# Eight weight pieces summed ahead for the half unit, all by VectorE, and one set of token parts from unit 2 on

## The chip, the cores and the metric

The kernel runs on one core of a Trainium2 chip. The metric is the device time of one execution, in microseconds (us). In the profile PE is TensorE (PEld its weight loads), DVE is VectorE, ACT is ScalarE, POOL is GpSimd and SP is SyncE. All times in the text without a unit are us, and times such as 598.83 count from the start of the span of the profiled execution.

## What is computed

Three stages follow each other: an attention with pooled keys, a mixture of experts with a capacity, and two plain layers over all 2304 tokens. The change is in the last stage, which uses 512 features and 2048 hidden units:

```python
h = x @ w_in            # 512 -> 2048
r = np.maximum(h, 0.0)
g = s * (r * r) + b
out = g @ w_out         # 2048 -> 512
```

A token that its expert had no room for enters the last stage as zeros, so its output row is known without a matmul. Only the kept tokens go through the two layers; the kernel learns their number on the chip.

## The kernel before

**Units.** `last_layers` takes the kept tokens in units of 256 (`CU`). Units 0 and 1 are interleaved in `pair`. Unit 2 is always run. Each later unit stands in a branch: `rest` asks whether more than `u * 256 + 128` tokens are kept and runs `unit(u)` if so; otherwise, if more than `u * 256` are kept, it runs `half(u)` for the last 128 or fewer. With these inputs units 0 to 4 run whole and a half unit ends the program.

**Precision.** A float32 operand is split into a high part `h` that TensorE takes at its fast rate and a low part `l`, and three products (hh, hl, lh) replace one. `w_in` lies in SBUF as 16 pieces `win[f]`, each a pair of high and low parts (in `w1h`/`w1l` for f below 8, in `w2h`/`w2l` above). The tokens of a unit come in as `yr`; `split_y` makes their parts, the high one on ACT (L1032), the low one by `eng` (L1033, POOL when `tokens(u + 1)` calls it). There are two sets of token parts in `x.yp`: set 0 in the tile `yhl`, set 1 in the tiles `y1h` and `y1l`.

**A whole unit.** The first layer makes 16 blocks of 128 hidden units, one for each piece: 12 matmuls into one of four PSUM banks (`ph`: tq, misc, bank2, bank3; L1040). `square` takes a bank by ACT (relu, L1424) and DVE (times itself, L1425) into one of four buffers `rt`; `parts` splits that, with the high part `gh` by ACT (L1439) and the low part `gl` by POOL (L1442, two instructions). Then the second layer runs over two blocks of 128 tokens (L1449), and `store` adds the bias on DVE (L1456) and scatters the rows with an indirect DMA from POOL (L1457).

**The half unit.** For 128 tokens the kernel doesn't use split operands in the first layer: it multiplies plain float32, four matmuls for each of the 16 pieces (L1568), which needs each piece of `w_in` whole. `whole(f)` sums its two parts into a slot (L1560, 128x512 elements). There are three slots, `raw2`, `raw3` and `c_f1`. Unit 2 fills them with pieces 0 to 2 ahead of its second layer, and `half` sums piece f + 3 into the slot of piece f as soon as the matmuls of f have read it. Of these sums the even ones go to DVE and the odd ones to POOL, where they stand between the low parts of `parts`. Each engine does its instructions in the order in which the code issues them.

**What orders the work.** The order is written out by hand (`manual_schedule`); the framework only adds the semaphores. `x.yr`, the four banks and the four `rt` are reused in rotation.

Of the kernel before, what the change touches and what calls it, by code (L numbers as in the profile page):

```python
# [7 lines left out]
F32 = mybir.dt.float32  # L8
# [12 lines left out]
DM = H * D  # L21
# [3 lines left out]
P = 128  # L25
# [864 lines left out]
class Experts:  # L890
# [137 lines left out]
        nc.sync.dma_start(out=self.it[u % 4], in_=self.idc[u * CU:u * CU + CU].rearrange("(j p) o -> p (j o)", p=P))  # L1028

    def split_y(self, u, k, eng):  # L1030
        h, l = self.yp[u % 2]
        self.nc.scalar.copy(h[:, k], self.yr[:, k])  # L1032
        eng.tensor_sub(l[:, k], self.yr[:, k], h[:, k])  # L1033

    def layer1_y(self, u, p, wh, wl):
        n = 0
        yh, yl = self.yp[u % 2]
        for k in range(KD):
            for l, r in ((wh, yh), (wh, yl), (wl, yh)):
                self.nc.tensor.matmul(p[:, :CU], lhsT=l[:, k], rhs=r[:, k], start=n == 0, stop=n == 3 * KD - 1)  # L1040
                n += 1
# [328 lines left out]
def last_layers(nc, tc, c, a, pool, side, x, ps, out):  # L1370
# [4 lines left out]
    w2h, w2l, it, kept, raw, rt = x.w2h, x.w2l, x.it, x.kept, x.raw, x.rt  # L1375
# [12 lines left out]
    sums, more, spare, slots = {}, [], [], []  # L1388

    v8 = lambda z: z.rearrange("p (k c) -> p k c", k=KD)  # L1390
    win = [(x.w1h[:, f], x.w1l[:, f]) for f in range(KF)] + [(v8(w2h[f]), v8(w2l[f])) for f in range(KF)]
# [22 lines left out]
    def conv(n, end=len(steps)):  # L1414
        for _ in range(n):
            if done[0] < end:
                z, i = steps[done[0]]
                z.step(i)
                done[0] += 1

    def square(f, p, n, inside=False):

        r = rt[f % 4][:, :n]
        nc.scalar.activation(r, p, AF.Relu)  # L1424
        nc.vector.scalar_tensor_tensor(out=p if inside else r, in0=p, scalar=0.0, in1=r, op0=ALU.max, op1=ALU.mult)  # L1425

    def place(f, u=0):

        if u != 1 or HEAD <= f < KF2 - 2:
            f -= HEAD if u == 1 else 0  # L1430
            return gh[:, f], gl[:, f]
        t = spare[f % (KF2 - 2)] if f < 3 or f > HEAD else more[(f - 3) // 2][:, (f - 3) % 2]
        return t[:, 0], t[:, 1]

    def parts(f, n=CU, u=0, p=None):

        h, l = place(f, u)
        r = rt[f % 4][:, :n] if p is None else p
        nc.scalar.copy(h[:, :n], r)  # L1439
        if p is None:  # L1440
            for z in (slice(0, n // 2), slice(n // 2, n)):
                nc.gpsimd.tensor_sub(l[:, z], r[:, z], h[:, z])  # L1442
        else:
            nc.vector.tensor_sub(l[:, :n], r, h[:, :n])

    def layer2(p, j, f, c=slice(0, DM), u=0):
        h, l = place(f, u)
        for i, (g, z) in enumerate(((h, 0), (h, 1), (l, 0))):
            nc.tensor.matmul(p[:, c], lhsT=g[:, j * P:j * P + P], rhs=wo[f][:, z, c], start=f == 0 and i == 0, stop=f == KF2 - 1 and i == 2)  # L1449
# [12 lines left out]
    def tokens(u):  # L1462
        if u < NV:
            for k in range(KD):
                x.split_y(u, k, nc.gpsimd)
# [8 lines left out]
    def load_out(i):  # L1474
        nc.sync.dma_start(out=wo[i].rearrange("p c two -> p (c two)"), in_=wout[:, i])

    def pair():

        for i in range(KF2 - 2):
            load_out(i)  # L1480
            if i == 5:
                x.load_y(1)
                for j, n in enumerate(("moe2_s", "moe2_b")):
                    nc.sync.dma_start(out=sb[:, j:j + 1], in_=a[n].unsqueeze(0).to_broadcast([P, 1]))
        more.extend(side.tile([P, 2, 2, CU], F32R, name=f"wo{i}") for i in range(KF2 - 2, KF2))
        spare.extend(x.w.tile([P, 2, CU], F32R, name=f"raw{i}") for i in range(3))
        held = []

        def first(u, f0, f1, banks):
            for n, f in enumerate(range(f0, f1)):  # L1490
                p = banks[f % len(banks)][:, :CU]
                if u or f >= EARLY:
                    x.layer1_y(u, p, *win[f])
                inside = f % 3 == 2
                square(f, p, CU, inside)
                conv(f < 6 or f % 2 if u == 0 else 1 if f < HEAD else 1 + f % 2, steps_of_first)
                if u == 0 and 7 <= f < 7 + KD:
                    x.split_y(1, f - 7, nc.vector)
                if held:
                    parts(*held.pop())  # L1500
                held.append((f, CU, u, p if inside else None))
            parts(*held.pop())

        def second(u, f0, f1, end):
            for f in range(f0, f1):
                for j in range(2):
                    layer2(po[2 * u + j], j, f, u=u)
                conv(1 if u and f < HEAD else 2, end)

        steps_of_first, all_steps = cvs[0].total, len(steps)  # L1510
        conv(2 * FIRST)
        nc.gpsimd.memset(onesf, 1.0)
        first(0, 0, KF2, ps)
        first(1, 0, HEAD, ph)
        x.load_y(2)
        second(0, 0, HEAD, steps_of_first)
        second(1, 0, HEAD, steps_of_first)
        for i in range(KF2 - 2, KF2):
            wo[i] = place_out(i, [P, DM, 2], I32)
            load_out(i)  # L1520
        first(1, HEAD, KF2, ph)
        second(0, HEAD, KF2, all_steps)
        tokens(2)
        second(1, HEAD, KF2, all_steps)
        conv(all_steps)
        raw[0:3] = [x.w.tile([P, DM], F32, name=f"raw{i}") for i in range(3)]
        slots.extend(raw[2:4] + [x.w.tile([P, DM], F32, name="c_f1")])
        sums["drop"] = x.w.tile([P, DM], F32, name="c_u0")

    def unit(u):  # L1530
        if u == 2:
            pair()
        if u + 1 < NV:
            x.load_y(u + 1)
        for f in range(KF2):
            p = ph[f % 4][:, :CU]
            x.layer1_y(u, p, *win[f])
            square(f, p, CU)
            if f:
                parts(f - 1)  # L1540
            if u == 2:
                if f == 1:
                    rows(ph[(f + 3) % 4])
                elif f > 11:
                    store((f - 12) // 2, f % 2, po[f - 12])
        parts(KF2 - 1)
        tokens(u + 1)
        if u == 2:
            for f in range(len(slots)):
                whole(f)  # L1550
        for j in range(2):
            p = po[2 * (u % 2) + j]
            for f in range(KF2):
                layer2(p, j, f)
            store(u, j, p)

    def whole(f):

        if f < KF2:
            (nc.gpsimd if f % 2 else nc.vector).tensor_add(v8(slots[f % len(slots)]), win[f][0], win[f][1])  # L1560

    def half(u):

        for f in range(KF2):
            p = ph[f % 4][:, :P]
            w = slots[f % len(slots)].rearrange("p (k c) -> p k c", k=KD)
            for k in range(KD):
                nc.tensor.matmul(p, lhsT=w[:, k], rhs=x.yr[:, k, 0:P], start=k == 0, stop=k == KD - 1)  # L1568
            square(f, p, P)
            whole(f + len(slots))  # L1570
            if f:
                parts(f - 1, P)
        parts(KF2 - 1, P)

        ids = x.ids_half
        for i in range(2):
            nc.vector.tensor_scalar(out=ids[:, i:i + 1], in0=it[u % 4][:, 0:1], scalar1=2, scalar2=i, op0=ALU.mult, op1=ALU.add)
        for i in range(2):
            c = slice(i * DM // 2, (i + 1) * DM // 2)
            p = po[2 * (u % 2) + i]  # L1580
            for f in range(KF2):
                layer2(p, 0, f, c)
            rows_out(raw[0], p, c, out.rearrange("t (i c) -> (t i) c", i=2), ids[:, i:i + 1])
# [67 lines left out]
```

## Time and profile before

| what | us |
|---|---|
| median of 3 runs | 645.44 |
| lowest and highest run | 642.06 and 647.37 |
| the profiled execution | 640.99 |
| its span, first to last instruction | 639.2 |
| the half unit, first matmul to the end of the span | 598.83 to 639.2 |

The mean granted TensorE clock of the profiled execution is 0.968 of full speed (2.4 GHz). A page gives averages over three different stages; what counts for the change is the last 40 us and the stretch from 443 to 466 in unit 2, so these are read from the timelines of each engine, where a number in brackets is idle time ahead of an instruction and the name behind it is what ended that.

### The profile page before, as it was taken

To read this page: it belongs to the slowest core of one execution; us is meant where nothing else is said; L and a number is where in the kernel's file an instruction comes from. 1 tells how busy PE (TensorE), PEld (TensorE's weight loads), DVE (VectorE), ACT (ScalarE), POOL (GpSimd) and SP (SyncE) were. 2 spreads that over 40 slices of the span, in tenths; PEclk is the share of its full clock that TensorE was granted. 3 is DMA by queue.
4 is the path that set the end of the run, shared out by engine and by line. 5 is a ranking of instruction groups with operands and counts; after the bars stand their busy time and mean duration, and the time that the engine had idled before them with its cause. 6 is when DMAs were issued, how large, how long until landed. Compare 5 with 4: busy or idle time off the path is not lost. (4 is left out here: it accounts for less than half of the span.)

```text
span 639.2 us, 11276 instructions
## 1 busy us (share of the span) xinstructions
PE 582.6 (91%) x4005; PEld 539.6 (84%) x4005; DVE 367.0 (57%) x893; ACT 250.0 (39%) x614; POOL 289.3 (45%) x486
## 2 busy tenths in 40 slices
PE   5788989699899979998899898999999999999885
PEld 5777878589899969997899787799899898898775
DVE  4687898887978966672669999324221031131140
ACT  1445655536456635525336534124033042041130
POOL 6557634716253806113237505227446055164391
PEclk8799999799899979999999999999999999999998
DMA  8999786636749893856587020145200101000000
GB/s 167 181 190 186 156 219 210 214 104 236 236 139 302 276 336 121 258 174 217 168 271 297 1 67 2 33 156 191 67 17 16 36 17 34 33 2 18 21 2 20
DMA packets 67951, 86.12 MB, mean 135 GB/s; under 512 B 24713, under 2 KB 40073, under 8 KB 67856
## 3 DMA queue, kind: packets, MB, share of 16 engines
q1 hardware_dynamic: 57168, 71.04, 37.7%
q10 hardware_dynamic: 8240, 7.14, 3.7%
q0 software_dynamic: 2448, 6.82, 3.4%
q8 instruction: 42, 0.69, 0.4%
q14 instruction: 53, 0.43, 0.2%
HBM read 68.09 MB, written 17.58 MB: 134 GB/s over the span
## 5 line engine op out<-in xcount | busy, mean ns | idle before, releaser
L1442 POOL TENSOR_TENSOR gl<-rt,gh 128x128 fp32r<-128x128 f32 (+1 forms) x192 | 89.3, 488 | 77.6 <-ACT gh L1439 77.4
L1449 PE MATMUL bank<-wo,gh 128*128 128x512 f32 (+1 forms) x340 | 99.8, 377 | 0.4 <-DVE wo L1400 0.4
L936 POOL TENSOR_TENSOR w1l<-kraw,w1h 128x128 fp32r<-128x128 f32 x96 | 51.6, 570 | 50.1 <-ACT w1h L929 50.1
L1113 PE MATMUL bank<-hs,w2h 128*128 128x288 f32 (+1 forms) x308 | 68.6, 311 | 5.1 <-issue 4.7
L1449 PEld LDWEIGHTS bank<-wo,gh 128*128 128x128 f32 x340 | 62.0, 188 | 13.4 <-DVE wo L1400 1.1
L1449 PE MATMUL bank<-wo,gl 128*128 128x512 f32 (+1 forms) x170 | 63.8, 375 | 0.0
L1456 DVE SCALAR_TENSOR_TENSOR raw<-bank,sb,c_u 128x512 f32<-128x512 f32 (+1 forms) x14 | 9.9, 711 | 85.6 <-PE bank L1449 85.6
L1113 PEld LDWEIGHTS bank<-hs,w2h 128*128 128x128 f32 x308 | 50.8, 192 | 6.1 <-issue 5.5
L1424 ACT ACTIVATE rt<-tq 128x256 f32<-128x256 f32 (+1 forms) x26 | 9.5, 367 | 111.7 <-PE tq L1040 89.0
L1113 PE MATMUL bank<-hs,w2l 128*128 128x288 f32 (+1 forms) x148 | 44.9, 303 | 0.0
L944 POOL DMA_INDIRECT xg<-xd,u_idx x23 | 26.1, 1135 | 35.8 <-DVE lt L294 16.4
L1425 DVE SCALAR_TENSOR_TENSOR rt<-bank,rt 128x256 f32<-128x256 f32 (+1 forms) x53 | 21.2, 400 | 36.5 <-ACT rt L1424 36.2
L1439 ACT CAST gh<-rt 128x256 fp32r<-128x256 f32 (+1 forms) x96 | 36.7, 382 | 11.3 <-DVE rt L1425 7.5
L1457 POOL DMA_INDIRECT out_dram<-raw,it x12 | 11.9, 994 | 62.8 <-DVE raw L1456 62.4
L1449 PEld LDWEIGHTS bank<-wo,gl 128*128 128x128 f32 x170 | 31.9, 188 | 6.4
L1424 ACT ACTIVATE rt<-bank 128x256 f32<-128x256 f32 (+1 forms) x60 | 22.3, 371 | 36.7 <-PE bank L1040 27.7
L230 PE MATMUL sc<-kbd,qT 128*128 128x144 f32 (+1 forms) x152 | 25.4, 316 | 6.4 <-DVE rmine L380 3.1
L967 PE MATMUL bank<-xs,w1h 128*128 128x288 f32 (+1 forms) x120 | 27.3, 313 | 2.1 <-DVE hs L970 2.1
L230 PEld LDWEIGHTS sc<-kbd,qT 128*128 128x128 f32 (+1 forms) x152 | 21.8, 200 | 8.5 <-issue 5.9
L1113 PEld LDWEIGHTS bank<-hs,w2l 128*128 128x128 f32 x148 | 28.4, 192 | 0.0
L1425 DVE SCALAR_TENSOR_TENSOR rt<-tq,rt 128x256 f32<-128x256 f32 (+1 forms) x24 | 9.6, 399 | 31.4 <-ACT rt L1424 31.4
L940 DVE TENSOR_TENSOR w2l<-vraw,w2h 128x512 fp32r<-128x512 f32 x39 | 26.8, 686 | 0.9 <-ACT w2h L939 0.5
(496 smaller groups left out, 1729.3 us busy)
## 6 DMA issues: line engine op xcount, KB each, us to landing
kraw<-in_moe_w_dram SPq DMA_DIRECT2D x14, 1024.0 KB
vraw<-in_moe_w_dram SPq DMA_DIRECT2D x14, 1024.0 KB
c_raw<-in_moe_w_in_dram ACTq DMA_DIRECT2D x13, 512.0 KB
wo<-in_moe_w_out_dram SPq DMA_DIRECT2D x13, 512.0 KB
kraw<-in_k_dram SPq DMA_DIRECT2D x8, 576.0 KB
out_dram<-c_u SPq DMA_DIRECT2D x1, 4608.0 KB
q<-in_q_dram SPq DMA_DIRECT2D x16, 256.0 KB
xd<-xr SPq DMA_DIRECT2D x16, 256.0 KB
```

The lines of the kernel that those rows point to most:

```text
L230: nc.tensor.matmul(sc[:n, p // 2, p % 2 * 144:p % 2 * 144 + 144], lhsT=q[:, p, :n], rhs=kbd[b % 2][:, p], start=True, stop=True)
L936: eng.tensor_sub(self.w1l[:, i, z], self.w1(i)[:, z], self.w1h[:, i, z])
L940: eng.tensor_sub(self.w2l[i], self.w2r[:, i], self.w2h[i])
L944: self.nc.gpsimd.indirect_dma_start(out=dst, out_offset=None, in_=self.xd[:have], in_offset=bass.IndirectOffsetOnAxis(ap=idx[:n], axis=0), ...
L967: self.nc.tensor.matmul(p, lhsT=l[:, f, k], rhs=r[k], start=n == 0, stop=n == 3 * KD - 1)
L1113: nc.tensor.matmul(py[d][:, :v.n], lhsT=l[f][:, d * P:d * P + P], rhs=r[f], start=f == 0 and i == 0, stop=f == KF - 1 and i == 2)
L1424: nc.scalar.activation(r, p, AF.Relu)
L1425: nc.vector.scalar_tensor_tensor(out=p if inside else r, in0=p, scalar=0.0, in1=r, op0=ALU.max, op1=ALU.mult)
L1439: nc.scalar.copy(h[:, :n], r)
L1442: nc.gpsimd.tensor_sub(l[:, z], r[:, z], h[:, z])
L1449: nc.tensor.matmul(p[:, c], lhsT=g[:, j * P:j * P + P], rhs=wo[f][:, z, c], start=f == 0 and i == 0, stop=f == KF2 - 1 and i == 2)
L1457: i = nc.gpsimd.indirect_dma_start(out=dst, out_offset=bass.IndirectOffsetOnAxis(ap=ids, axis=0), in_=o[:, c], in_offset=None, bounds_chec ...
```

## The change

Eight slots replace three: `c_f0`, `c_f1`, the storage of `y1h` and `y1l` cut into two slots each, and `raw2`, `raw3`. Unit 2 sums pieces 0 to 7 ahead, and the half unit sums pieces 8 to 15, all on DVE. To free the storage of `y1h` and `y1l`, set 1 of the token parts serves unit 1 alone; units 2 and later all use set 0. The low part in `parts` is cut in pieces of 128 columns, which is as before for 256 tokens and is one instruction rather than two for the 128 of the half unit.

```diff
--- before.py
+++ after.py
@@ -1028,13 +1028,13 @@
         nc.sync.dma_start(out=self.it[u % 4], in_=self.idc[u * CU:u * CU + CU].rearrange("(j p) o -> p (j o)", p=P))
 
     def split_y(self, u, k, eng):
-        h, l = self.yp[u % 2]
+        h, l = self.yp[u == 1]
         self.nc.scalar.copy(h[:, k], self.yr[:, k])
         eng.tensor_sub(l[:, k], self.yr[:, k], h[:, k])
 
     def layer1_y(self, u, p, wh, wl):
         n = 0
-        yh, yl = self.yp[u % 2]
+        yh, yl = self.yp[u == 1]
         for k in range(KD):
             for l, r in ((wh, yh), (wh, yl), (wl, yh)):
                 self.nc.tensor.matmul(p[:, :CU], lhsT=l[:, k], rhs=r[:, k], start=n == 0, stop=n == 3 * KD - 1)
@@ -1438,8 +1438,8 @@
         r = rt[f % 4][:, :n] if p is None else p
         nc.scalar.copy(h[:, :n], r)
         if p is None:
-            for z in (slice(0, n // 2), slice(n // 2, n)):
-                nc.gpsimd.tensor_sub(l[:, z], r[:, z], h[:, z])
+            for z in range(0, n, P):
+                nc.gpsimd.tensor_sub(l[:, z:z + P], r[:, z:z + P], h[:, z:z + P])
         else:
             nc.vector.tensor_sub(l[:, :n], r, h[:, :n])
 
@@ -1524,7 +1524,11 @@
         second(1, HEAD, KF2, all_steps)
         conv(all_steps)
         raw[0:3] = [x.w.tile([P, DM], F32, name=f"raw{i}") for i in range(3)]
-        slots.extend(raw[2:4] + [x.w.tile([P, DM], F32, name="c_f1")])
+        slots.extend(x.w.tile([P, DM], F32, name=f"c_f{i}") for i in range(2))
+        for n in "hl":
+            z = pool.tile([P, 2, DM], F32, name=f"y1{n}")
+            slots.extend(z[:, i] for i in range(2))
+        slots.extend(raw[2:4])
         sums["drop"] = x.w.tile([P, DM], F32, name="c_u0")
 
     def unit(u):
@@ -1557,7 +1561,7 @@
     def whole(f):
 
         if f < KF2:
-            (nc.gpsimd if f % 2 else nc.vector).tensor_add(v8(slots[f % len(slots)]), win[f][0], win[f][1])
+            nc.vector.tensor_add(v8(slots[f % len(slots)]), win[f][0], win[f][1])
 
     def half(u):
```

The first place is DVE in unit 2, from the last two stores of unit 1 to the branch behind the unit (`raw` and `c_f` are slots here, L1560 of before is L1564 of the changed kernel). Before:

```order
L1456 SCALAR_TENSOR_TENSOR raw2_17954<-bank6_1946,sb_17059,c_u0_17956 128x512
L1425 SCALAR_TENSOR_TENSOR rt3_1971<-bank3_1943,rt3_1971 128x256
L1456 SCALAR_TENSOR_TENSOR raw3_1963<-bank7_1947,sb_17059,c_u0_17956 128x512
L1560 TENSOR_TENSOR raw2_17954<-w1h_144,w1l_145 128x512
L1560 TENSOR_TENSOR c_f1_17955<-w1h_144,w1l_145 128x512
L1456 SCALAR_TENSOR_TENSOR raw0_17952<-bank4_1944,sb_17059,c_u0_17956 128x512
L1456 SCALAR_TENSOR_TENSOR raw1_17953<-bank5_1945,sb_17059,c_u0_17956 128x512
```

And now:

```order
L1456 SCALAR_TENSOR_TENSOR raw2_17954<-bank6_1946,sb_17059,c_u0_17959 128x512
L1425 SCALAR_TENSOR_TENSOR rt3_1971<-bank3_1943,rt3_1971 128x256
L1456 SCALAR_TENSOR_TENSOR raw3_1963<-bank7_1947,sb_17059,c_u0_17959 128x512
L1564 TENSOR_TENSOR c_f0_17955<-w1h_144,w1l_145 128x512
L1564 TENSOR_TENSOR c_f1_17956<-w1h_144,w1l_145 128x512
L1564 TENSOR_TENSOR y1h_17957<-w1h_144,w1l_145 128x512 x2
L1564 TENSOR_TENSOR y1l_17958<-w1h_144,w1l_145 128x512 x2
L1564 TENSOR_TENSOR raw2_17954<-w1h_144,w1l_145 128x512
L1564 TENSOR_TENSOR raw3_1963<-w1h_144,w1l_145 128x512
L1456 SCALAR_TENSOR_TENSOR raw0_17952<-bank4_1944,sb_17059,c_u0_17959 128x512
L1456 SCALAR_TENSOR_TENSOR raw1_17953<-bank5_1945,sb_17059,c_u0_17959 128x512
```

Six more sums stand between the stores of unit 1 and those of unit 2, and the sum that wrote `raw2` first now stands last but one.

The second place is DVE in the half unit that runs, from its branch on (`rt` are the squares, L1425). Before:

```order
L1599 COMPARE_AND_BRANCH
L1425 SCALAR_TENSOR_TENSOR rt0_1968<-tq_1607,rt0_1968 128x128
L1425 SCALAR_TENSOR_TENSOR rt1_1969<-misc_1608,rt1_1969 128x128
L1560 TENSOR_TENSOR raw3_1963<-w1h_144,w1l_145 128x512
L1425 SCALAR_TENSOR_TENSOR rt2_1970<-bank2_1942,rt2_1970 128x128
L1425 SCALAR_TENSOR_TENSOR rt3_1971<-bank3_1943,rt3_1971 128x128
L1560 TENSOR_TENSOR raw2_17954<-w1h_144,w1l_145 128x512
L1425 SCALAR_TENSOR_TENSOR rt0_1968<-tq_1607,rt0_1968 128x128
L1425 SCALAR_TENSOR_TENSOR rt1_1969<-misc_1608,rt1_1969 128x128
```

And now:

```order
L1603 COMPARE_AND_BRANCH
L1425 SCALAR_TENSOR_TENSOR rt0_1968<-tq_1607,rt0_1968 128x128
L1564 TENSOR_TENSOR c_f0_17955<-w2h0_146,w2l0_147 128x512
L1425 SCALAR_TENSOR_TENSOR rt1_1969<-misc_1608,rt1_1969 128x128
L1564 TENSOR_TENSOR c_f1_17956<-w2h0_146,w2l0_147 128x512
L1425 SCALAR_TENSOR_TENSOR rt2_1970<-bank2_1942,rt2_1970 128x128
L1564 TENSOR_TENSOR y1h_17957<-w2h_1951,w2l_1952 128x512
L1425 SCALAR_TENSOR_TENSOR rt3_1971<-bank3_1943,rt3_1971 128x128
L1564 TENSOR_TENSOR y1h_17957<-w2h_1951,w2l_1952 128x512
L1425 SCALAR_TENSOR_TENSOR rt0_1968<-tq_1607,rt0_1968 128x128
```

Before, a sum stood behind every second square, and the slot that it wrote was read three pieces later; now one stands behind each of the first eight squares, and the slot that it writes is read eight pieces later.

The third place is POOL in the half unit (`gl` are the low parts). Before:

```order
L1599 COMPARE_AND_BRANCH
L1560 TENSOR_TENSOR raw2_17954<-w1h_144,w1l_145 128x512
L1442 TENSOR_TENSOR gl_17067<-rt0_1968,gh_17066 128x64 x2
L1560 TENSOR_TENSOR c_f1_17955<-w1h_144,w1l_145 128x512
L1442 TENSOR_TENSOR gl_17067<-rt1_1969,gh_17066 128x64 x2
L1442 TENSOR_TENSOR gl_17067<-rt2_1970,gh_17066 128x64 x2
L1560 TENSOR_TENSOR raw3_1963<-w1h_144,w1l_145 128x512
L1442 TENSOR_TENSOR gl_17067<-rt3_1971,gh_17066 128x64 x2
L1442 TENSOR_TENSOR gl_17067<-rt0_1968,gh_17066 128x64 x2
```

And now:

```order
L1603 COMPARE_AND_BRANCH
L1442 TENSOR_TENSOR gl_17067<-rt0_1968,gh_17066 128x128
L1442 TENSOR_TENSOR gl_17067<-rt1_1969,gh_17066 128x128
L1442 TENSOR_TENSOR gl_17067<-rt2_1970,gh_17066 128x128
L1442 TENSOR_TENSOR gl_17067<-rt3_1971,gh_17066 128x128
L1442 TENSOR_TENSOR gl_17067<-rt0_1968,gh_17066 128x128
L1442 TENSOR_TENSOR gl_17067<-rt1_1969,gh_17066 128x128
```

Seven sums have left POOL's row, and the low part of each block is one instruction.

## Rows read from the trace of the kernel before

**Rows 1.** The chain that ended last, from 601 to 605: start, us, what.

```profile
601.03 1.64 issue
...
602.88 1.42 POOL raw L1560
...
604.34 1.30 PE bank L1568 x8
```

**Rows 2.** Timeline of PE, half unit: start, us, instruction, [idle before <-releaser].

```profile
598.83 1.05 PE L1568 MATMUL tq<-yr,raw 128*128 128x128 f32 x8
...
604.34 1.30 PE L1568 MATMUL bank<-yr,raw 128*128 128x128 f32 x8 [2.67 <-POOL raw L1560]
...
608.75 1.95 PE L1568 MATMUL bank<-yr,raw 128*128 128x128 f32 x16
610.53 1.06 PE L1568 MATMUL tq<-yr,c_f 128*128 128x128 f32 x8
...
620.31 1.16 PE L1568 MATMUL bank<-yr,raw 128*128 128x128 f32 x8 [0.73 <-POOL raw L1560]
621.22 0.48 PE L1449 MATMUL bank<-c_raw,gh 128*128 128x256 f32 x2
```

**Rows 3.** Windows: length, busy us of PE, PEld, DVE, ACT, POOL, PEclk, DMA share, GB/s.

```profile
606.00:609.00 3.00, 3.00 (x18) 3.00 (x17) 1.18 (x3) 0.68 (x4) 3.00 (x7) 0.56 0.00 0
...
615.00:618.00 3.00, 2.27 (x20) 2.08 (x20) 2.11 (x5) 0.93 (x4) 3.00 (x6) 1.00 0.00 0
```

**Rows 4.** Timeline of POOL, half unit.

```profile
602.88 1.41 POOL L1560 TENSOR_TENSOR raw<-w1h,w1l 128x512 f32<-128x512 f32 x1 [1.84 <-ACT rt L1424]
...
608.88 1.80 POOL L1442 TENSOR_TENSOR gl<-rt,gh 128x64 fp32r<-128x64 f32 x4
...
613.43 1.26 POOL L1560 TENSOR_TENSOR c_f<-w2h,w2l 128x512 f32<-128x512 f32 x1
...
622.12 1.16 POOL L1442 TENSOR_TENSOR gl<-rt,gh 128x64 fp32r<-128x64 f32 x4 [0.20 <-ACT gh L1439]
```

**Rows 5.** Timeline of DVE, half unit.

```profile
602.28 0.29 DVE L1425 SCALAR_TENSOR_TENSOR rt<-misc,rt 128x128 f32<-128x128 f32 x1 [1.61 <-ACT rt L1424]
602.48 0.68 DVE L1560 TENSOR_TENSOR raw<-w1h,w1l 128x512 f32<-128x512 f32 x1
603.08 0.28 DVE L1425 SCALAR_TENSOR_TENSOR rt<-bank,rt 128x128 f32<-128x128 f32 x1
...
609.55 0.68 DVE L1560 TENSOR_TENSOR c_f<-w2h,w2l 128x512 f32<-128x512 f32 x1
...
613.76 1.48 DVE L1560 TENSOR_TENSOR raw<-w2h,w2l 128x512 f32<-128x512 f32 x1
```

**Rows 6.** Timeline of ACT, half unit.

```profile
600.90 0.28 ACT L1424 ACTIVATE rt<-misc 128x128 f32<-128x128 f32 x1 [0.62 <-PE misc L1568]
```

**Rows 7.** Timeline of POOL, end of unit 2 and start of unit 3.

```profile
448.04 0.90 POOL L1442 TENSOR_TENSOR gl<-rt,gh 128x128 fp32r<-128x128 f32 x2
448.88 3.77 POOL L1033 TENSOR_TENSOR y1l<-yr,y1h 128x256 fp32r<-128x256 f32 x4
...
469.06 0.87 POOL L1442 TENSOR_TENSOR gl<-rt,gh 128x128 fp32r<-128x128 f32 x2 [1.69 <-ACT gh L1439]
```

**Rows 8.** Timeline of POOL, end of the first layer of unit 4.

```profile
579.35 2.81 POOL L1033 TENSOR_TENSOR yhl<-yr,yhl 128x256 fp32r<-128x256 f32 x4
```

**Rows 9.** Timeline of DVE, second layer of unit 2.

```profile
447.79 1.71 DVE L1560 TENSOR_TENSOR raw<-w1h,w1l 128x512 f32<-128x512 f32 x1 [3.02 <-DMA out_dram<-raw,it]
...
454.28 0.75 DVE L1456 SCALAR_TENSOR_TENSOR raw<-bank,sb,c_u 128x512 f32<-128x512 f32 x1 [3.64 <-PE bank L1449]
465.38 0.75 DVE L1456 SCALAR_TENSOR_TENSOR raw<-bank,sb,c_u 128x512 f32<-128x512 f32 x1 [10.34 <-PE bank L1449]
```

**Rows 10.** Timeline of PE, second layer of unit 2 and the start of unit 3.

```profile
453.85 0.39 PE L1449 MATMUL bank<-wo,gl 128*128 128x512 f32 x1
...
465.18 0.28 PE L1040 MATMUL tq<-y1h,w1h 128*128 128x256 f32 x1
```

## The prediction

> **What bounds the kernel now.** I read the chain that ended last first, backwards from the end. Where the half unit begins it runs over POOL: 1.64 in which POOL waited for nothing shown, a sum of two weight parts (L1560) of 1.42, and only then TensorE [rows 1]. So the place is the half unit's first layer. Its 16 pieces run from 598.83 to 621.22, 22.39 us [rows 2]. A piece that waits for nothing takes 0.89 (two from 608.75 to 610.53), so 16 of them need 14.24. **8.1 us are lost**, and TensorE's rows say to what: 2.67 idle before the fourth piece until POOL's sum had ended, later 0.73 before every second piece for the same reason [rows 2], and slow pieces in between, as the granted clock fell to 0.56 (near the 1.2 GHz level) in 606 to 609 after the long wait and was back at 1.00 later [rows 3].
>
> Why POOL is late: its timeline is without a gap from 602.88 to 623.28 [rows 4]. Of the 13 sums that the half unit makes, the seven odd ones are POOL's, about 1.26 each, with the low parts of two blocks between them. That is a period of about 2.8 for two pieces where TensorE needs 1.78. DVE takes 0.68 for the same sum when nothing blocks it [rows 5] and has gaps.
>
> **The change, part by part.**
>
> *Sums leave POOL in the half unit.* Seven sums go, 7 × 1.26 = 8.8 of POOL's time. The low part of a block becomes one instruction of 128 columns, which costs 0.44 (0.87 for two in unit 3 [rows 7]) in place of 2 × 0.29 (1.16 for four at the very end [rows 4]). POOL's load per piece falls to 0.44 against TensorE's 0.89, so POOL stops being the bound.
>
> *Eight slots instead of three.* Pieces 0 to 7 are ready before the half unit starts, so no TensorE wait for a sum is left there. Piece 8 + k is summed right behind square k. On DVE a square costs 0.20 to the next issue (602.28 to 602.48) and a sum 0.60 (602.48 to 603.08) [rows 5]: 0.80 per piece, below 0.89. A sum has eight pieces, 7.1 us, of lead over its reader; all eight take 6.4. What is late next is not the sum but the *square behind it*: it frees the PSUM bank for the piece four later. If DVE starts no earlier than in this trace (602.28), square k ends at about 602.4 + 0.8k, and piece k + 4 can start on time at 598.83 + 0.89 × (k + 4) = 602.4 + 0.89k: just ahead for k = 1 and further ahead after. The first layer then ends at 598.83 + 14.24 = 613.1, 8.1 earlier, and the clock has no long wait to fall after.
>
> *Who follows.* The second layer reads the low parts. In this trace the last of them was ready at 623.28, 2.06 after that layer had begun [rows 2, 4], and TensorE didn't wait; POOL, less loaded, will not be later. Second layer, last store and drain (621.22 to 639.2) only move forward.
>
> *Unit 2 makes eight sums on DVE, not two, and POOL one less.* DVE waited 3.02 for a scatter to land before it could write raw2, and idled 3.64 and 10.34 before the unit's two stores [rows 9]. Now the first six slots wait for nothing, so the sums start at 444.8 and need 8 × 0.68 = 5.4 free, or 8 × 1.71 = 13.7 if all are blocked like the first in this trace. They end between 450.2 and 458.5. The store behind them, at 454.28, may slip by 4.2; its bank is next wanted two units later, and DVE's next task is at 465.38. Cost 0. For POOL: beside two DVE sums its four token parts took 3.77, without them 2.81 [rows 7, 8], so 0.48 lost per sum, 8 × 0.48 = 3.9. POOL's last low part of the unit ends at 448.94 and TensorE wants it at 453.85, 4.9 later [rows 7, 10]; the token parts, 452.65 + 3.9 = 456.5, are wanted at 465.18. Cost 0, with 1.0 to spare in the worse place.
>
> *One set of token parts.* The parts of unit u + 1 are now written over those of unit u. They are made behind the last square of unit u, which itself waited for the last matmul that reads them. The wait that this adds is already over: 0. The 128-column cut leaves 256-token units as they are.
>
> *Sum.* At most 8.1. TensorE's wait at 601.5 to 604.34 also hid whatever its own code might have come late by; DVE, behind the same branch, got going again only at 602.28, so 0 to 0.8 may show up there. I take the middle, 0.4. **Gain 7.7**: the profiled execution would be 640.99 − 7.7 = 633.3 and the median 645.44 − 7.7 = **637.7**. (The profiled execution lies 4.45 under the median of the runs; I carry the gain over to the median, as the half unit is the same work in each run.)
>
> **The port.** DVE's sum at 613.76 took 1.48, not 0.68: POOL's sum ran from 613.43 to 614.69, and DVE's ended 0.55 after that. But the sum at 609.55, amid four low parts, took 0.68, and those four took 1.80 rather than 1.16 [rows 4, 5]. So either may hold the other up. The Trainium skill ("SBUF — State Buffer", Who interferes with whom) says just this: a VectorE instruction with two SBUF inputs and a GpSimd instruction that reads SBUF exclude each other for a whole instruction, whoever comes first. It speaks against giving every sum to DVE while POOL keeps its low parts: were POOL always first, the gain would be the first rival's 5.3; were DVE always first, the forecast's 7.7. The trace bears out both orders.
>
> **Rivals.**
>
> *DVE becomes the bound.* If each sum finds a low part in flight it costs 0.60 + 0.44, and with the square 1.24 per piece, over TensorE's 0.89. Then square 8, behind eight sums, ends at 602.28 + 8 × 1.24 + 0.1 = 612.3, pieces 12 to 15 follow it, and the layer ends at 612.3 + 4 × 0.89 = 615.9: gain 5.3. POOL also starts with up to two low parts of backlog, 0.9: gain 4.4. If DVE isn't late at the start (from 600.67), 6.9. Time 638.5 to 641.0, say 639.3. For it: the row at 613.76. Against it: a low part can start only after ACT has read the square, when DVE's sum is already running, as at 609.55.
>
> *The code behind the branch comes late.* DVE had its relu at 601.18 [rows 6] and was free, yet squared at 602.28; POOL stood 1.64 with nothing to wait for [rows 1]. If TensorE or DVE loses another such 1.6 where no wait covers it: gain 6.1, time 639.3. The Trainium skill ("Runtime: NRT & Kernel Launch", Instruction fetch mechanics) says that a taken branch out of the loaded window forces a fetch; this trace has the delay but doesn't prove the cause. Code sizes shift by a few instructions, so it may fall elsewhere.
>
> *Slower: unit 2's sums starve POOL.* If each of the eight kept POOL out for the 1.71 that the longest lasted, the last low part would come at 448.94 + 13.7 = 462.6, 8.8 after TensorE wants it; with the slow clock after such a wait (1.7 in the half unit: three pieces from 604.34 in 4.41, not 2.68) 10.5 are lost and 7.7 gained: 648.2. It decides from 4.9 lost by POOL on, and turns the sign from about 11. Against it: the measured 0.48 per sum.
>
> *It doesn't do what it says:* the slots are there but a reader still waits, as for a slot's old content. Unit 2's sums have 140 us of lead, so only the second eight could; no time gained, 645.
>
> **How the numbers follow.** About 1% (6.45 us) is what a measurement can tell from no change here, and 7.7 is 1.2%. Chances: forecast (gain 7.3 to 8.1) 0.62; DVE bound 0.18; late code 0.12; nothing gained 0.05; slower 0.03. The forecast lands over 1% in some 85 of 100 cases, given runs that spread by 5.3; the next two in about 40. Faster 0.62 × 0.85 + 0.30 × 0.4 = 0.65, slower 0.03, same 0.32. Range: from 637.3 less the 3.4 by which the lowest run before lay under the median, 633.9, to DVE's worst, 641.0. All of it is one sign.
>
> **What would show it.** Right: no L1560 (now L1564) row on POOL; 16 pieces in 14.2 to 15 us with granted clock 1.00; POOL with gaps in the half unit; sums of 0.6 to 1.2. Wrong: TensorE waiting on a square (DVE) between pieces 5 and 12; a gap before the fourth piece with no engine to wait for; a TensorE wait on POOL's low parts near 453 in unit 2. It would also be wrong if the stages ahead of unit 2, which the change leaves alone, moved.

## The result and the profile after

| | median, us | runs | ratio to before (95% interval) |
|---|---|---|---|
| before | 643.91 | 642.06 to 647.37 | |
| changed | 634.71 | 633.17 to 636.45 | 0.9862 (0.9827 to 0.9897) |

The kernel is 8.9 us faster (643.91 × 0.0138), with an interval of 6.6 to 11.1. Two later sets of runs of the same kernel gave 0.9836 (0.9787 to 0.9886) and 0.9916 (0.9885 to 0.9948); the three, weighted by the inverse square of their interval's width, make 0.9882, a gain of 7.6. The forecast was 7.7.

One count ahead of the prediction is off by one: units 0 to 5 run whole, the half unit is number 6, and [rows 8] are of unit 5. No term depends on it.

The profiled execution of the changed kernel took 635.53 us (span 633.8). The chain that ended last no longer passes through POOL in the half unit's first layer (start, us, what); compare [rows 1].

```profile
600.82 0.92 PE tq L1572 x8
...
602.63 1.79 PE bank L1572 x16
...
613.45 1.80 PE bank L1572 x16
```

The timeline of TensorE in the half unit, as [rows 2], shows why: the 16 pieces run from 600.65 to 614.99, 14.34 us instead of 22.39. No row has idle time in front; at 604.25, the fifth piece, the wait for the first square's bank costs some 0.1.

```profile
600.65 1.08 PE L1572 MATMUL tq<-yr,c_f 128*128 128x128 f32 x8
...
604.25 1.16 PE L1572 MATMUL tq<-yr,y1l 128*128 128x128 f32 x8
...
613.29 1.95 PE L1572 MATMUL bank<-yr,raw 128*128 128x128 f32 x16
614.99 0.48 PE L1449 MATMUL bank<-c_raw,gh 128*128 128x256 f32 x2
```

The windows of that stretch (length, busy us of PE, PEld, DVE, ACT, POOL, granted clock, DMA share, GB/s) answer to [rows 3]: TensorE is busy throughout, the granted clock stays at 1.00 (the 2.4 GHz level), and of the other engines DVE is now the fullest.

```profile
604.20:608.00 3.80, 3.80 (x35) 3.77 (x35) 3.80 (x9) 2.17 (x10) 2.11 (x4) 1.00 0.01 4
608.00:612.00 4.00, 4.00 (x38) 4.00 (x38) 3.64 (x10) 2.44 (x12) 2.45 (x5) 1.00 0.00 0
```

POOL in the half unit, as [rows 4]: low parts of 0.45 to 0.62, with gaps, the last one done at 617.17, 2.18 after the second layer began.

```profile
604.77 0.45 POOL L1442 TENSOR_TENSOR gl<-rt,gh 128x128 fp32r<-128x128 f32 x1 [1.91 <-ACT rt L1424]
605.46 0.62 POOL L1442 TENSOR_TENSOR gl<-rt,gh 128x128 fp32r<-128x128 f32 x1 [0.24 <-PE tq L1572]
...
607.29 0.52 POOL L1442 TENSOR_TENSOR gl<-rt,gh 128x128 fp32r<-128x128 f32 x1 [0.35 <-PE bank L1572]
...
616.71 0.46 POOL L1442 TENSOR_TENSOR gl<-rt,gh 128x128 fp32r<-128x128 f32 x1 [0.32 <-POOL gl L1442]
```

DVE in the half unit, as [rows 5]: its first square stands 2.30 idle, though the relu that it needs ended at 602.14; from there it runs through its eight sums without a gap, 0.80 to 0.98 per piece and mostly 0.86. A sum starts shortly before POOL's low part ends (607.62, the low part at 607.29 + 0.52 = 607.81).

```profile
603.91 0.29 DVE L1425 SCALAR_TENSOR_TENSOR rt<-tq,rt 128x128 f32<-128x128 f32 x1 [2.30 <-ACT rt L1424]
604.11 0.68 DVE L1564 TENSOR_TENSOR c_f<-w2h,w2l 128x512 f32<-128x512 f32 x1
604.71 0.28 DVE L1425 SCALAR_TENSOR_TENSOR rt<-misc,rt 128x128 f32<-128x128 f32 x1
...
607.62 0.74 DVE L1564 TENSOR_TENSOR y1l<-w2h,w2l 128x512 f32<-128x512 f32 x1
```

Unit 2, as [rows 9]: DVE's sums start at 446.79 without a wait. The last waits 1.25 for a scatter to land, then takes 2.82. The first store behind the sums isn't late even so: DVE was free 0.18 before TensorE let it start.

```profile
446.79 1.28 DVE L1564 TENSOR_TENSOR c_f<-w1h,w1l 128x512 f32<-128x512 f32 x2
...
451.21 0.95 DVE L1564 TENSOR_TENSOR raw<-w1h,w1l 128x512 f32<-128x512 f32 x1
453.40 2.82 DVE L1564 TENSOR_TENSOR raw<-w1h,w1l 128x512 f32<-128x512 f32 x1 [1.25 <-DMA out_dram<-raw,it]
456.40 0.75 DVE L1456 SCALAR_TENSOR_TENSOR raw<-bank,sb,c_u 128x512 f32<-128x512 f32 x1 [0.18 <-PE bank L1449]
```

POOL there, as [rows 7]: the last low parts end at 452.89, the token parts at 455.67.

```profile
451.57 1.32 POOL L1442 TENSOR_TENSOR gl<-rt,gh 128x128 fp32r<-128x128 f32 x2
452.86 2.81 POOL L1033 TENSOR_TENSOR yhl<-yr,yhl 128x256 fp32r<-128x256 f32 x4
```

TensorE there, as [rows 10]: the second layer of unit 2 runs from 445.09 to 467.29, 22.20 as before (442.98 to 465.18).

```profile
445.09 0.63 PE L1449 MATMUL bank<-c_raw,gh 128*128 128x512 f32 x2
...
467.29 0.40 PE L1040 MATMUL tq<-yhl,w1h 128*128 128x256 f32 x2
```

So the layer gave 22.39 − 14.34 = 8.05. The two profiled executions differ by only 5.4 in span, as the one after reached unit 2's second layer 2.1 later, and its end came 18.8 after the layer instead of 18.0. Over all profiles of this study that second layer begins anywhere between 441.3 and 450.5, in stages that no kernel here changed, and the end comes 18.0 to 20.1 after the layer. That is enough to account for the spread of the runs, and for why medians of few runs differ by 2 to 3; what moves these stages is open. (It need not all be chance: both profiles of the kernel with two cuts have 449.9, the three of the changed kernel 441.3 to 445.1.)

### The profile page after: what moved, and what is told of

It reads as the page before. It is cut to its first block, busy times and chain, and to the rows that moved or that the text cites. A ratio compares the mean times of both kernels' runs of the same rounds, so it can differ in the third digit from the quotient of the medians.

```text
span 633.8 us, 11287 instructions
## 1 busy us (share of the span) xinstructions
PE 583.3 (92%) x4005; PEld 540.7 (85%) x4005; DVE 371.0 (59%) x901; ACT 249.4 (39%) x614; POOL 277.2 (44%) x462
## 5 line engine op out<-in xcount | busy, mean ns | idle before, releaser
L1442 POOL TENSOR_TENSOR gl<-rt,gh 128x128 fp32r<-128x128 f32 x176 | 87.5, 519 | 84.0 <-ACT gh L1439 79.7
L1439 ACT CAST gh<-rt 128x256 fp32r<-128x256 f32 (+1 forms) x96 | 36.7, 383 | 17.4 <-DVE rt L1425 11.1
L1425 DVE SCALAR_TENSOR_TENSOR rt<-bank,rt 128x256 f32<-128x256 f32 (+1 forms) x53 | 21.2, 400 | 31.9 <-ACT rt L1424 31.8
L1040 PE MATMUL bank<-yhl,w2h 128*128 128x256 f32 x176 | 32.2, 284 | 1.1 <-DVE gl L1444 1.1
L1040 PE MATMUL bank<-yhl,w1h 128*128 128x256 f32 x176 | 31.0, 279 | 0.0
L1425 DVE SCALAR_TENSOR_TENSOR rt<-tq,rt 128x256 f32<-128x256 f32 (+1 forms) x24 | 9.6, 400 | 32.9 <-ACT rt L1424 32.8
L1040 PEld LDWEIGHTS bank<-yhl,w2h 128*128 128x128 f32 x176 | 27.4, 192 | 1.2 <-DVE gl L1444 1.2
```

The source lines that it names most:

```text
L1442: nc.gpsimd.tensor_sub(l[:, z:z + P], r[:, z:z + P], h[:, z:z + P])
```

## The experiments

The layer is the time from the half unit's first matmul to the first of its second layer, from one profile each; the ratio is that of timed runs to the kernel before, on the same chip.

| kernel | layer, us | ratio (95% interval) |
|---|---|---|
| before | 22.39 | |
| changed, again | 14.38 | 0.9836 (0.9787 to 0.9886) |
| changed, a third time | 14.45 | 0.9916 (0.9885 to 0.9948) |
| three slots | 16.96 | 0.991 (0.9876 to 0.9945) |
| four slots | 15.08 | 0.9931 (0.9898 to 0.9964) |
| odd sums on POOL | 15.30 | 0.9918 (0.9884 to 0.9952) |
| two cuts per low part | 15.40 | 0.9933 (0.9907 to 0.9959) |
| two cuts, again | 15.41 | 0.9918 (0.9887 to 0.9949) |
| sums twice in the half unit | 20.68 | 0.9974 (0.9938 to 1.0011) |
| sums twice in unit 2 | 14.26 | 0.9851 (0.9824 to 0.9879) |
| no half units 7 and 8 | 14.20 | 0.9902 (0.986 to 0.9944) |
| before, with the single cut alone | 21.14 | 0.9981 (0.9951 to 1.0012) |

The ratios follow the layers only roughly, since a layer is known to 0.1 us and a ratio to some 2 us; the layers decide below.

**The changed kernel again.** No edit.

> The changed kernel again, for a second profile and a narrower ratio. Theory (the half unit's first layer is TensorE-bound now): that layer takes 14.2 to 14.6 us again, 8 less than before, and the ratio to the kernel before is 0.986 to 0.990. If a good part of the gain came from stages ahead of unit 2, the layer would take the same but the ratio would leave that range.

The layer took 14.38. The ratio, 0.9836, lies just under the range that was named, and its interval reaches into it. The third set:

> The changed kernel once more on the chip that runs the two others of this batch. Theory: first layer of the half unit 14.3 to 14.5 us; the ratio to the kernel before 0.984 to 0.990, since what is left of the spread comes from stages ahead of the last layers, which reach their second layer anywhere between 356 and 366 us in the profiles so far.

14.45 and 0.9916, this time above the range. The layer repeats to 0.1, the ratio to 0.008, so the ratio can't decide whether a part of the gain came from stages ahead of unit 2. The profiles say more: from unit 2's second layer to the half unit it took 155.56 in each of the three, 155.85 before.

**Three slots.**

```diff
-        slots.extend(x.w.tile([P, DM], F32, name=f"c_f{i}") for i in range(2))
-        for n in "hl":
-            z = pool.tile([P, 2, DM], F32, name=f"y1{n}")
-            slots.extend(z[:, i] for i in range(2))
-        slots.extend(raw[2:4])
+        slots.extend(raw[2:4] + [x.w.tile([P, DM], F32, name="c_f1")])
```

> The changed kernel with three slots again (raw2, raw3, c_f1); all sums stay on DVE, so unit 2 makes three and the half unit thirteen. Theory: POOL's sums were the bound, and DVE alone keeps up in steady state (sum f + 3 ends about 1.4 us after piece f, TensorE wants it after 1.8), so the slots only cover DVE's late start: sum 3 is ready some 4.1 us into the layer instead of 2.7, one wait of about 1.4 us, and the layer takes 15.6 to 16.5 us, 1.2 to 2 more than with eight slots. Rival (the lead of eight pieces is what pays): a wait at every piece, the layer at 18 us or more, over half of the gain gone.

16.96, between the two theories' numbers. The one long wait is there, on TensorE's timeline before the fourth piece, and it is DVE's now:

```profile
602.53 1.16 PE L1568 MATMUL bank<-yr,raw 128*128 128x128 f32 x8 [1.53 <-DVE raw L1560]
```

But the theory that DVE keeps up afterwards failed: its period is 0.97 (nine pieces from 605.32 to 614.04, sums of 0.77 to 0.97 beside the low parts), over TensorE's 0.89, and with thirteen sums that goes on to the end.

```profile
605.32 0.28 DVE L1425 SCALAR_TENSOR_TENSOR rt<-tq,rt 128x128 f32<-128x128 f32 x1
...
614.04 0.28 DVE L1425 SCALAR_TENSOR_TENSOR rt<-misc,rt 128x128 f32<-128x128 f32 x1
```

So taking the sums off POOL gives 5.4 of the 8.0 together with the single cut, which is in this kernel too (alone it gives 1.25, below), and the slots the rest: they cover DVE's late start and leave DVE eight sums instead of thirteen.

**Four slots, two token sets.**

```diff
-        for n in "hl":
-            z = pool.tile([P, 2, DM], F32, name=f"y1{n}")
-            slots.extend(z[:, i] for i in range(2))
         slots.extend(raw[2:4])
```
```diff
-        h, l = self.yp[u == 1]
+        h, l = self.yp[u % 2]
...
-        yh, yl = self.yp[u == 1]
+        yh, yl = self.yp[u % 2]
```

> The changed kernel with the two sets of token parts by turns again, so that y1h and y1l stay in use and only four slots are left (c_f0, c_f1, raw2, raw3); twelve sums in the half unit, all on DVE. Theory (slots cover DVE's late start and the 0.95 to 1.0 us that DVE takes per piece as long as sums last): sum 4 is ready 4.1 us into the layer, wanted at 3.6, and some eleven further pieces go at DVE's pace: layer of 15.6 to 16.4 us, between the 14.4 of eight slots and the 17.0 of three. Units 3 and 5, which read set 1 again, take 0.14 us longer each than unit 4. Rival (one more slot is enough to hide all): 14.4 us.

15.08, below the range that was expected: one wait of 0.51 for sum 4, then DVE's period is 0.86 and TensorE, 0.5 behind, runs on without another. Why DVE needs 0.86 here and 0.97 with three slots was not tested.

```profile
604.97 1.16 PE L1569 MATMUL tq<-yr,c_f 128*128 128x128 f32 x8 [0.51 <-DVE c_f L1561]
```

Units 3 and 5 took 22.40 for their first layer and unit 4 22.26, as expected. So one slot more than three gives 1.9 of the layer (16.96 to 15.08), and the four further ones 0.7 (to 14.38).

**Odd sums on POOL again.**

```diff
-            nc.vector.tensor_add(v8(slots[f % len(slots)]), win[f][0], win[f][1])
+            (nc.gpsimd if f % 2 else nc.vector).tensor_add(v8(slots[f % len(slots)]), win[f][0], win[f][1])
```

> The changed kernel with eight slots, but the odd sums on POOL again: four in the half unit. Theory (POOL's load is the cause): POOL has 4 x 1.3 + 8 x 0.45 to 0.55 us in the first eight pieces and starts about 4.1 us late; the sums still come ahead of their readers, but low parts come late, relu waits for the rt buffer that a low part still reads, and TensorE for the bank: 0.5 to 1.5 us more than the changed kernel, layer of 15 to 16 us. Rival (eight slots alone are enough): no wait, layer 14.4 us, the same time as the changed kernel within 0.2 per cent. Rival (taking the sums off POOL is all): layer over 18 us.

15.30, the first theory. No sum is late; TensorE waits for a low part, by way of relu, which can't reuse rt before POOL has read it, and the bank:

```profile
610.22 1.13 PE L1572 MATMUL bank<-yr,y1h 128*128 128x128 f32 x8 [0.51 <-POOL gl L1442]
```

POOL's period is 2.5 for two pieces, a sum of 1.29 and two low parts of 1.34 together:

```profile
608.03 1.29 POOL L1564 TENSOR_TENSOR y1l<-w2h,w2l 128x512 f32<-128x512 f32 x1
609.26 1.34 POOL L1442 TENSOR_TENSOR gl<-rt,gh 128x128 fp32r<-128x128 f32 x2
```

DVE's first square was on time in this run, so none of this is its late start. Both this kernel and the one with three slots have the single cut, so their base is the 21.14 of the kernel before with that cut: eight slots give 5.8 on top of it, DVE alone 4.2, and both together 6.8 (14.38). A late sum isn't needed for POOL to delay the layer.

**The half unit's sums twice.**

```diff
             whole(f + len(slots))
+            whole(f + len(slots))
```

> The changed kernel with each of the half unit's eight sums done twice on DVE; the second writes the same values, so nothing is left out. Theory (DVE has little to spare, the square behind each sum frees the bank): DVE's period per piece is 0.20 + 2 x 0.60 + 0.14 = 1.54 us for eight pieces, square 8 ends about 15.7 us into the layer, four more pieces follow it, and the layer takes about 19.3 us: 5 us slower than the changed kernel, 3 us faster than before. Rival (DVE is far from being the bound): under 2 us slower.

20.68: the mechanism is the expected one, the size 1.4 off. TensorE waits before eight of the pieces, and each time for a square, not a sum:

```profile
612.62 1.16 PE L1572 MATMUL tq<-yr,c_f 128*128 128x128 f32 x8 [0.51 <-DVE rt L1425]
```

On DVE a square and its two sums take 1.67 (612.28 to 613.95), against 1.54 expected; the pair alone takes 1.54.

```profile
612.28 0.28 DVE L1425 SCALAR_TENSOR_TENSOR rt<-tq,rt 128x128 f32<-128x128 f32 x1
612.48 1.54 DVE L1564 TENSOR_TENSOR y1l<-w2h,w2l 128x512 f32<-128x512 f32 x2
613.95 0.28 DVE L1425 SCALAR_TENSOR_TENSOR rt<-misc,rt 128x128 f32<-128x128 f32 x1
```

This is the first rival's mechanism, seen at work: if DVE takes longer per piece than TensorE, the square behind the sum holds the bank. In the changed kernel, with DVE's 0.86 against TensorE's 0.89, it doesn't.

**The single cut.**

```diff
-            for z in range(0, n, P):
-                nc.gpsimd.tensor_sub(l[:, z:z + P], r[:, z:z + P], h[:, z:z + P])
+            for z in (slice(0, n // 2), slice(n // 2, n)):
+                nc.gpsimd.tensor_sub(l[:, z], r[:, z], h[:, z])
```

> The changed kernel with the low part of a half unit's block in two instructions of 64 columns again. Theory: POOL needs 0.57 to 0.85 us per piece instead of 0.45 to 0.52, still below 0.89, and its rows stay ahead of the rt buffers: layer of 14.3 to 14.7 us, no difference that can be measured. If the single cut carried part of the gain, the layer would take over 15 us.

15.40, a miss: 1.0 more than the changed kernel. POOL's first low part starts 6.03 into the layer, not 4.12, after 3.83 of idle time (the name behind it is no cause: that ended long before).

```profile
611.51 11.44 POOL L1442 TENSOR_TENSOR gl<-rt,gh 128x64 fp32r<-128x64 f32 x32 [3.83 <-PE misc L1572]
```

DVE then waits 0.80 for a relu that waits for rt, and TensorE for banks:

```profile
612.84 0.29 DVE L1425 SCALAR_TENSOR_TENSOR rt<-tq,rt 128x128 f32<-128x128 f32 x1 [0.80 <-ACT rt L1424]
```

The same kernel was run again to see whether this was chance:

> The changed kernel with two cuts per low part again, a second time, as its first run had POOL's first low part 1.9 us later than in the changed kernel and a layer of 15.4 us, which was not expected. Theory (POOL's code comes late at a fixed place of its instruction stream, which the 16 added instructions move): the same 3.8 us of idle time on POOL and the same layer of 15.4 us; if it was chance, 14.4 us.

15.41, and POOL's row is the same to 0.01:

```profile
611.52 11.44 POOL L1442 TENSOR_TENSOR gl<-rt,gh 128x64 fp32r<-128x64 f32 x32 [3.83 <-PE misc L1572]
```

It is no chance. POOL's branch into the half unit (L1603) ran at 609.1, 3.6 into the layer as in the changed kernel (604.3), so the further 1.9 lie behind the branch. That the cause is the place of POOL's code is what the theory says, and the fixed delay fits; it was not shown by itself, nor how much of the 1.0 comes from the late start and how much from POOL's larger load per piece. The same cut was also put into the kernel before, alone:

> The kernel before with one part of the change alone: the low part of a half unit's block is one instruction of 128 columns. Three slots, odd sums on POOL, two token sets. Theory (POOL's load sets the pace of the half unit's first layer): POOL's period for two pieces falls from about 2.8 us (a sum of 1.26 and four cuts of 0.4) to about 2.3 (a sum and two cuts of 0.5), six or seven periods, so the layer takes 19 to 20.5 us instead of 22.4. Rival (the lead of three pieces, not POOL's load): the layer stays at 22 us or more.

21.14, between the two theories' numbers: POOL's load does set the pace there, by less than expected. The period of two pieces is 2.51 (the POOL sums at 613.21 and 615.72), since two low parts beside a sum on DVE take 1.32, not 1.0. TensorE's later waits for POOL's sum are 0.46 instead of 0.73 [rows 2]. The long wait before the fourth piece stays at 2.67 though, so that one isn't POOL's load: POOL's first instruction comes some 4.0 into the layer in both kernels (603.33 − 599.32 here, 602.88 − 598.83 before), late behind the branch.

```profile
613.21 1.26 POOL L1560 TENSOR_TENSOR c_f<-w2h,w2l 128x512 f32<-128x512 f32 x1
614.44 1.32 POOL L1442 TENSOR_TENSOR gl<-rt,gh 128x128 fp32r<-128x128 f32 x2
```

```profile
604.83 1.16 PE L1568 MATMUL bank<-yr,raw 128*128 128x128 f32 x8 [2.67 <-POOL raw L1560]
...
617.04 1.16 PE L1568 MATMUL misc<-yr,raw 128*128 128x128 f32 x8 [0.46 <-POOL raw L1560]
```

**Nearer code.** Half units 7 and 8 are left out, which these inputs don't reach.

```diff
-            with tc.If(kept > u * CU):
-                half(u)
+            if u < 7:
+                with tc.If(kept > u * CU):
+                    half(u)
```

> The changed kernel without the branches for half units 7 and 8, which these inputs don't reach (it leaves them out and would be wrong for other inputs); so the code of the half unit that runs stands nearer to the branch that leads to it. Theory (DVE's and POOL's idle time at the start of the half unit is code that comes late): DVE's first square starts within 0.6 us of its relu, not 2.0 to 2.4 us after; the layer takes 14.2 to 14.4 us, as TensorE hardly waited for it, so the time stays within 0.3 per cent of the changed kernel. If that idle time were something that POOL or DVE waits for in the program, it would stay.

The layer took 14.20. On DVE the idle time is 0.59 and ends with the relu that its square needs, though each engine executes the same instructions as in the changed kernel:

```profile
599.29 0.29 DVE L1425 SCALAR_TENSOR_TENSOR rt<-tq,rt 128x128 f32<-128x128 f32 x1 [0.59 <-ACT rt L1424]
```

On POOL it stayed, against the expectation:

```profile
601.90 6.08 POOL L1442 TENSOR_TENSOR gl<-rt,gh 128x128 fp32r<-128x128 f32 x9 [1.96 <-ACT rt L1424]
```

So DVE's 2.30 was nothing that it waits for in the program. The branch instructions, which the timelines leave out, say where it stood. In the changed kernel DVE took the outer branch behind unit 5 at 600.9, and the inner one, which is the first instruction at the place jumped to, came at 603.7 (each line gives count, shortest, median and longest duration in ns, and the first and last start; the half unit's are the last of L1599 and the first of L1603):

```profile
L1599 DVEq COMPARE_BRANCH  x4: 43/46/63, 467.5 to 600.9; - x4
L1603 DVEq COMPARE_BRANCH  x2: 43/45/47, 603.7 to 626.6; - x2
```

Here the same two are 0.5 apart, not 2.8:

```profile
L1599 DVEq COMPARE_BRANCH  x4: 43/46/62, 464.6 to 598.0; - x4
L1604 DVEq COMPARE_BRANCH  x2: 43/45/47, 598.5 to 623.6; - x2
```

POOL's inner branch came 3.6 to 3.9 into the layer in every profile of this study, the kernel before among them; its part stays open. The ratio, 0.9902, gives no gain for DVE's punctual start.

**Unit 2's sums twice.**

```diff
                 whole(f)
+                whole(f)
```

> The changed kernel with each of unit 2's eight sums done twice (same values). Theory (POOL loses about 0.25 us per sum there and has slack): POOL's last low part of the unit comes 9 to 10 us into the second layer, wanted at 10.9; no wait of TensorE, second layer of unit 2 at 22.2 us, same time as the changed kernel within 0.3 per cent. Rival (the slower case: the sums starve POOL): a TensorE wait on a low part near the end of the first block of that layer, of 1 us or more.

No TensorE wait anywhere in units 2 to 5, and the layer took 14.26. It was DVE that lost: four sums took 6.53 as POOL's last low parts and its four token parts ran past them, and the store behind came at 467.58, hidden all the same.

```profile
455.82 6.53 DVE L1565 TENSOR_TENSOR y1h<-w1h,w1l 128x512 f32<-128x512 f32 x4
...
467.58 0.74 DVE L1456 SCALAR_TENSOR_TENSOR raw<-bank,sb,c_u 128x512 f32<-128x512 f32 x1
```

POOL's own rows are as short as without any sum (2.81 in [rows 8]), and its last low part came 6.5 into the second layer, earlier than in the changed kernel (7.8):

```profile
456.06 0.89 POOL L1442 TENSOR_TENSOR gl<-rt,gh 128x128 fp32r<-128x128 f32 x2
456.90 2.83 POOL L1033 TENSOR_TENSOR yhl<-yr,yhl 128x256 fp32r<-128x256 f32 x4
```

The slower rival's mechanism, POOL starved by sums, is not there at twice the number. A side effect: with eight more instructions ahead of it in DVE's code, the half unit's first square was on time, as in the run without half units 7 and 8.

```profile
607.62 0.29 DVE L1425 SCALAR_TENSOR_TENSOR rt<-tq,rt 128x128 f32<-128x128 f32 x1 [0.65 <-ACT rt L1424]
```

## Why the prediction was right

**The bound.** That POOL bounds the half unit's first layer held from both sides: with less load on POOL alone the layer fell to 21.14, with all sums off POOL as well to 16.96, and with eight slots but four sums left there it was 15.30. One reading was too simple: the prediction explains POOL's lateness by its load, but the 2.67 before the fourth piece comes from POOL's late start, as it stayed at 2.67 with the smaller load. The eight slots remove that wait too, so the sum didn't suffer.

**The sum.** Forecast: 14.24 for 16 pieces, a loss of 8.1, less 0.4 for code that might come late. Measured: 14.34 to 14.45, a gain of 7.9 to 8.05. The term for late code was mis-sized, 0.1 to 0.2 instead of 0.4: DVE did come late, but its first square started 3.26 into the layer (603.91 − 600.65) where the prediction's sum had allowed for 3.45, and the four banks cover that to the tenth. TensorE wasn't late: it had no gap ahead of its first piece.

**DVE's period.** Put at 0.80, measured at 0.86, as its sums take 0.74 beside low parts of 0.52. This is nearer to the trace's unblocked row than to the full block that the first rival was priced at (1.24): a sum starts 0.19 before a low part ends and ends some 0.20 after the next has begun, and in these overlaps sum and low part lost 0.06 or 0.07 each. The Trainium skill ("SBUF — State Buffer", Who interferes with whom) has the two exclude each other for a whole instruction. The trace doesn't speak against it: whoever comes second can lose only what is left of the other's instruction, here 0.2, and in unit 2 a sum lost 2.1 to a row of them. So the price of a collision goes by what is left and what is queued on the other engine.

**Unit 2.** The bounds for a blocked sum, 0.68 to 1.71, were too narrow above: one took 2.82. Those for POOL were safe: its last low part came 7.80 into the second layer (452.89 − 445.09) instead of 5.96 (448.94 − 442.98), so it lost 1.84 where up to 3.9 was allowed. TensorE waited for neither, so the term of 0 held.

**The token sets.** Put at 0, they gave 0.14 in unit 3 and in unit 5 each (22.40 to 22.26). This step was wrong by 0.28, and is the last section's matter.

**The 128-column cut** was right as a smaller load, but the prediction didn't see that it also goes with when POOL's first low part comes: with two cuts that was 1.9 later and the layer 1.0 longer.

**The median.** 637.7 was forecast and 634.7 came. The trace accounts for 8.05 + 0.28 = 8.3. The first set's 8.9, with an interval from 6.6 to 11.1, holds that, and so do the three sets together (7.6, with a third that reads 5.4). The 3 us between the forecast median and the measured one are then mostly spread: the median before was given as 645.44 and came out at 643.91 with one run more. That the median fell into the range, 633.9 to 641.0, owes something to luck, as the second set's, 633.75, would not have; and the profiled execution, forecast at 633.3, took 635.53. What was right is the layer: its bound, its sum and the gain of 8.

**The rivals.** DVE as the bound appeared when its sums were doubled and, with 0.97 per piece, with three slots, but not in the changed kernel; a late start appeared on DVE and POOL, but cost TensorE only the tenth; nothing starved POOL in unit 2.

## What to carry to other kernels

Where an engine waits for short jobs that are dealt out to two others, look at the row of the slower of the two as a whole: its other work counts against the same period, and moving its share to a faster engine with gaps (4.2 us here, on top of the single cut) and a deeper buffer (5.8) each give most of what both give together (6.8), so the two are not to be added up. A buffer ahead pays twice, by covering a late start (here behind a branch) and by taking jobs out of the stretch that is short of time. What stands behind a job on its engine, here the square that frees a bank, is what the next shortage delays.

## What the runs showed that I had not expected

**A matmul's time goes with the pair of tiles that it reads.** In the kernel before, between 465 and 601, the groups of TensorE's instructions (line, operation, names, count, then busy us, mean ns of one) show tokens in y1h with pieces in w1h at 282 ns and in w2h at 276, and tokens in yhl the other way round. All are 128x256 at clock 1.00.

```profile
L1040 PE MATMUL bank<-y1h,w1h 128*128 128x256 f32 x32 | 9.0, 282 | 0.0
...
L1040 PE MATMUL bank<-y1h,w2h 128*128 128x256 f32 x32 | 8.8, 276 | 0.0
...
L1040 PE MATMUL bank<-yhl,w2h 128*128 128x256 f32 x32 | 5.8, 283 | 0.0
L1040 PE MATMUL bank<-yhl,w1h 128*128 128x256 f32 x32 | 5.5, 276 | 0.0
```

A first layer takes 22.40 with set 1 and 22.26 with set 0. The run with four slots, where odd units use set 1 again, shows it again. Why isn't known; no run placed a tile elsewhere on purpose.

**Where code stands seems to move an engine's start by 2 us.** Behind the branch to the half unit DVE lost 1.1 in the kernel before (second square at 602.28, relu done at 601.18), 1.8 in the changed one (first square at 603.91 against 602.14), and nothing in three runs: without half units 7 and 8, with unit 2's sums twice, and with the odd sums on POOL. POOL's first low part moved by 1.9 with 16 instructions more in the half unit. The Trainium skill ("Runtime: NRT & Kernel Launch", Instruction fetch mechanics) says that code is fetched in blocks, the next one ahead in sequence, and that a taken branch out of the loaded blocks stalls. The run without half units 7 and 8 agrees for DVE: the instructions that it executes, the data and the waits were those of the changed kernel, only the code that isn't executed changed, and the 2.3 vanished between a branch and the first instruction at its target. That the time went into fetching, and how large a block is, no run shows.

**A DVE sum can lose to a whole row of POOL instructions.** In unit 2 of the changed kernel it started at 453.40 and ended at 456.22, 0.55 after the last of four token parts that ran from 452.86 to 455.67. The sum of the kernel before at 613.76 also ended 0.55 after POOL's [rows 4, 5].
